# An adaLN attention and gated-mixer block on one core: projections stage with paired modulation sums, output projection with seven held tiles, mixing in the common ring

## The chip, the cores and the metric

The kernel runs on one core of one Trainium2 chip. The metric is the device time of one execution in microseconds (us); less is better. Three runs of the kernel before took 1479.3, 1481.84 and 1483.68 us, and their median, 1481.84 us, is the time that a change is held against.

## What is computed

The reference, cut to what matters (S = 2048 rows, D = 448 columns, 16 heads of 28, Fh = 896; all float32):

```python
mod = (silu(c) @ w_mod).reshape(1, 6, 1, D)          # sa, ca, ga, sb, cb, gb
h = layernorm(x) * (1 + ca) + sa
q, k, v = split_heads(h @ wqkv)
p = softmax(q @ k.T / sqrt(28))                      # per head, 2048 x 2048
x = x + ga * (merge_heads(p @ v) @ wo)
h = layernorm(x) * (1 + cb) + sb
z = gelu(h @ w_in)                                   # 2048 x 1792
z1, z2 = z[:, :Fh], layernorm(z[:, Fh:])
g = w_sp @ z2 + b_sp[:, None]                        # w_sp: 2048 x 2048
out = x + gb * ((z1 * g) @ w_out)
```

## The kernel before

The kernel is written with a manual schedule: on each engine the instructions run in the order in which the program issues them, and nothing reorders them. TensorE's operands are split into a high and a low part, so a float32 product is made of several single-pass matmuls. `weight_part` (L76) and `ln_transpose` (L96) make the parts: the high one by a cast on ScalarE or VectorE, the low one by a subtraction (`sub`, L69) on GpSimd or VectorE. A product over D = 448 takes the 11 steps of `STEPS` (L31): 9 of `STEPS_MAIN`, which need the columns 0 to 383, and 2 of `STEPS_Z`, which need the columns 384 to 447 (part c = 3).

Rows are handled in 16 tiles of 128, four to a group. The stages, in order:

1. **Projections** (L169 to L311). `x` is loaded group by group, `w_mod` in six column blocks (`load_mod`, L145), each turned into a sum over k on VectorE (`mod_acc`, L185) and into columns or a broadcast row by matmuls (`mod_col`, L193; `mod_bc`, L199). For each group, `ln_stats` and `ln_norm` (L206, L219) normalise on VectorE with the reciprocal root on GpSimd, `ln_transpose` transposes on TensorE, `v_tile` (L237) makes V, and `qk_unit` (L244) makes 128 rows of q or k for the group and stores their high and low parts in DRAM (`qk_scr`). Seven row blocks m of q and k times four groups make 28 such units; 8 of them (m = 0 and 3) run within the group loop.
2. **Start of attention.** When the group loop has ended, its memory is freed (`early.close()`), the tiles `kst` and `qst` for three heads are made, the rows of ones in `kst` are written by three DMAs (L330), and `load_head` (L334) reads the heads 0 and 1 from DRAM. 20 more `qk_unit`s follow. The first 4 have nothing between their matmuls; into the other 16, 80 score matmuls for the row maxima (`m_mm`, L343, each followed by a VectorE reduction of 512 columns, L351) are laid, 5 to a unit.
3. **Attention loop** over 256 steps u = (head, key tile): 4 score matmuls (`s_mm`, L374) with their exponentials on ScalarE, 4 `m_mm` for 20 steps later, and the products with V (`pv_mm`, L387). A softmax sum comes out as row 28 of each block of 32 rows. After each head `n_copy`, `n_sum`, `n_recip`, `n_bcast`, `n_mul` and `n_scatter` (L398 to L433) bring the sums through DRAM to a broadcast reciprocal, multiply, and put the head's rows into `OT`. For the last head this chain runs after the loop (`run_tail`).
4. **Output projection and second norm** (L555 to L670). The `STEPS_MAIN` of 12 tiles run first and are added to `x`, while the last head's chain runs; then `o_split` (L435) splits its rows and the `STEPS_Z` of these tiles follow in small batches, each with a second addition. Norms (`h2_stats`, `h2_norm`, L585, L595) and `h2_group` go in between; the last-written parts of each group's `ln_transpose` go to VectorE.
5. **First half of the gated layer**: 28 `z1_unit`s (L669), with the later groups' norms between them; then the **second half**, `z2_gemm` (L737) per tile.
6. **Mixing** (`mix_part`, L787): 1344 matmuls into seven accumulators, then `gate` (L807) and the output product `y_part` (L825).

PSUM has 8 banks. `ring` holds 7 of them, used in turn by all stages up to the mixing, and `ps_o` one. Before the mixing both are closed, and `ps_f` gives the eight banks fixed names (acc0 to acc6, y_ps).

SyncE issues nearly all DMAs, in program order; each issue also waits until the eighth DMA before it has landed.

Of the kernel before, what the change touches and what calls it, by code (L numbers as in the profile page):

```python
# [20 lines left out]
NG = 4  # L21
# [12 lines left out]
def tile_adaln_mha_gmlp(ctx, tc, x, wqkv, wo, w_in, w_spT, b_sp, w_out, cT, w_mod, out):  # L34
# [17 lines left out]
    dve.memset(ones, 1.0)  # L52
    mhalf = const.tile([128, 4], F32, name="mhalf")
# [42 lines left out]
    def ln_transpose(xns, full_pool, dsts, scol, bcol, engs, los=(pool,) * 4, mid=None):  # L96
# [9 lines left out]
        for c in (0, 2, 1, 3):  # L106
# [13 lines left out]
            if c < 3:  # L120
                sub(los[c], dsts[:, 3 + c, :], f, hi)
            else:
                sub(los[c], hi[64:128], f[64:128], hi[64:128])

# [14 lines left out]
    early = ExitStack()  # L139
    e1 = early.enter_context(tc.tile_pool(name="e1", bufs=2))  # L140

    wv = e1.tile([128, 8, D], F32R, name="wv", bufs=1)
    wms, xts, raws = {}, {}, {}

    def load_mod(i, nm, eng):  # L145
        wm = e1.tile([112, 4, D], F32, name="wm")
        eng.dma_start(wm, w_mod[:, i * D : (i + 1) * D].rearrange("(k p) d -> p k d", p=112))
        wms[nm] = wm

    def load_x(g, eng):  # L150
        xg = e1.tile([128, 4, D], F32, name="xg")
        for t0, t1 in ((0, 1), (1, 2), (2, 4)) if g == 0 else ((0, 4),):
            eng.dma_start(
                xg[:, t0:t1, :], x[g * 512 + t0 * 128 : g * 512 + t1 * 128].rearrange("(t p) d -> p t d", p=128)
            )
        for t in range(4):
            xts[4 * g + t] = xg[:, t, :]
# [13 lines left out]
    load_mod(1, "ca", sp)  # L171
    load_mod(0, "sa", sp)
    for i in range(4):
        load_w("v", i, sp)
# [10 lines left out]
    def mod_acc(nm):  # L185
        acc = e1.tile([112, D], F32, name="acc")
        wm = wms[nm]
        dve.tensor_scalar(out=acc, in0=wm[:, 0, :], scalar1=silu[:, 0:1], scalar2=None, op0=ALU.mult)
        for k in range(1, 4):
            dve.scalar_tensor_tensor(out=acc, in0=wm[:, k, :], scalar=silu[:, k : k + 1], in1=acc, op0=ALU.mult, op1=ALU.add)  # L190
        return acc

    def mod_col(nm, acc, plus1):  # L193
        pc = ps_o.tile([128, 512], F32, name="pc", tag="o")
        for c, r, e in ((0, 0, 128), (1, 0, 128), (2, 0, 128), (3, 0, 64), (3, 64, 128)):
            pe.matmul(pc[r:e, c : c + 1], acc[:, c * 128 : c * 128 + e - r], ones[:112, 0:1], start=True, stop=True)
        return lambda: dve.tensor_scalar(out=cols[nm], in0=pc[:, 0:4], scalar1=plus1, scalar2=None, op0=ALU.add)

    def mod_bc(nm, acc):  # L199
        pc = ps_o.tile([128, 512], F32, name="pc", tag="o")  # L200
        pe.matmul(pc[:, :D], ones[:112, :], acc, start=True, stop=True)
        dve.tensor_copy(bcs[nm], pc[:, :D])
# [34 lines left out]
    def v_tile(kt):  # L237
        g, t = divmod(kt, 4)
        pv = ring.tile([128, 512], F32, name="pv", tag="s")
        for j, (a, b) in enumerate(STEPS):  # L240
            pe.matmul(pv[:, :D], hT[g][:, a, t * 128 : (t + 1) * 128], wv[:, b, :], start=j == 0, stop=j == NST - 1)
        dve.tensor_copy(V[:, kt, :, 0:DH], pv[:, :D].rearrange("p (h d) -> p h d", d=DH))
# [16 lines left out]
    ln_stats(0)  # L259
    xns = ln_norm(0)  # L260
    acc_ca = mod_acc("ca")
    acc_sa = mod_acc("sa")
    for i in range(4):
        weight_part(wv, i, raws["v", i], act, pool, False)
    ad = (act, act, dve, dve)

    def mod_first():
        col_ca = mod_col("ca", acc_ca, 1.0)
        col_ca()
        mod_col("sa", acc_sa, 0.0)()  # L270

    ln_transpose(
        xns, e1, hT[0], cols["ca"], cols["sa"], ad, (pool, pool, dve, dve), mod_first,
# [4 lines left out]
    pool.memset(V[:, :, :, DH:32], 1.0)  # L278
    ln_stats(1)
    xns = ln_norm(1)  # L280
    for g in range(NG):
        if g + 2 < NG:
            load_x(g + 2, sp)
        if g == 0:
            load_mod(2, "ga", sp)
            load_mod(3, "sb", sp)
        v_tile(4 * g)
        v_tile(4 * g + 1)
        if g == 0:
            for i in range(4):  # L290
                weight_part(wqk, i, raws["qk", i], act, (dve, pool)[i % 2], False)
        if g + 1 < NG:
            ln_transpose(xns, e1, hT[g + 1], cols["ca"], cols["sa"], (act,) * 4)
        v_tile(4 * g + 2)
        if g == 3:
            mod_col("sb", acc_b, 0.0)()
            acc_b = mod_acc("gb")
        v_tile(4 * g + 3)
        if g == 3:
            mod_col("cb", acc_a, 1.0)()  # L300
        if g + 2 < NG:
            ln_stats(g + 2)
        for m in (0, 3):
            qk_unit(m, g)
        if g + 2 < NG:
            xns = ln_norm(g + 2)
        if g == 1:
            acc_a = mod_acc("ga")
            load_mod(4, "cb", sp)
            acc_b = mod_acc("sb")  # L310
            load_mod(5, "gb", sp)  # L311
        if g == 2:
            mod_bc("ga", acc_a)
            acc_a = mod_acc("cb")
        if g == 3:
            mod_bc("gb", acc_b)
    early.close()


    stk = att.enter_context(tc.tile_pool(name="stk", bufs=1))  # L320
    ppool = att.enter_context(tc.tile_pool(name="ppool", bufs=6))
    kst = [stk.tile([128, S], F32R, name=f"kst{i}") for i in range(3)]
    qst = [stk.tile([128, S], F32R, name=f"qst{i}") for i in range(3)]
    npool = att.enter_context(tc.tile_pool(name="npool", bufs=2))
# [3 lines left out]

    for i in range(3):
        sp.dma_start(  # L330
# [578 lines left out]
```

## Time and profile before

| | us |
|---|---|
| median of three runs | 1481.84 (1479.3 to 1483.68) |
| the profiled execution | 1484.28 |
| its span, from the first to the last instruction | 1482.5 |
| TensorE matmul busy in it | 1444.3 |
| VectorE, ScalarE, GpSimd busy | 891.8, 723.7, 294.2 |
| mean granted TensorE clock | 0.994 of full |

The page of the profile gives the busy time of each engine (PE is TensorE's matmuls, PEld its weight loads, DVE VectorE, ACT ScalarE, POOL GpSimd, SP SyncE, SPq its DMA issues), then 40 equal slices of the span. Other views group instructions by line, list who waited for whom, give the busy time in chosen stretches, or list instructions in order of time: start, duration, engine, line, operation, count, and in brackets the idle time before it and what ended it. Busy matmuls are modelled to the end of their pipeline, so that neighbours overlap; the distance between starts is the real pace.

### The profile page before, as it was taken

What the parts mean: (1) busy time and instruction counts of PE and PEld (TensorE: products, weight loads), DVE (VectorE), ACT (ScalarE), POOL (GpSimd) and SP (SyncE); (2) the same over time, 40 slices, a digit from 0 to 9 for tenths busy, and PEclk for the clock granted to TensorE, in tenths of its full rate; (3) what the DMA queues carried; (4) which work ended last, traced back from release to release, by engine and by line L of the source; (5) the groups of instructions that cost most, each with busy time, mean ns of one, the idle gap of its engine ahead of it and who ended that gap; (6) DMA issues with size and microseconds to landing.
All of it is one profiled execution on the core that took longest, in us unless ns stands there. A gap on an engine that the chain in (4) does not pass through costs nothing. (4 is left out here: it accounts for less than half of the span.)

```text
span 1482.5 us, 19584 instructions
## 1 busy us (share of the span) xinstructions
PE 1444.3 (97%) x7284; PEld 1014.8 (68%) x7284; DVE 891.8 (60%) x1469; ACT 723.7 (49%) x1374; POOL 294.2 (20%) x282
## 2 busy tenths in 40 slices
PE   4998999999999999999999999999999999999999
PEld 3886755555555555555555547778988888888887
DVE  6726888888888888888888821752541411413114
ACT  3522467677677676776776784343432210211111
POOL 4723300000002011101000021540763300302002
PEclk8999999999999999999999999999999999999999
DMA  9336402210122112221022004632003322323223
GB/s 233 107 108 203 151 17 52 52 41 25 40 52 52 39 35 57 52 48 43 16 51 52 12 20 122 206 111 100 8 21 102 114 75 68 106 62 101 84 68 106
DMA packets 58790, 111.57 MB, mean 75 GB/s; under 512 B 12006, under 2 KB 27462, under 8 KB 56006
## 3 DMA queue, kind: packets, MB, share of 16 engines
q1 hardware_dynamic: 58534, 109.40, 25.9%
q8 instruction: 57, 0.93, 0.3%
q0 software_dynamic: 160, 0.92, 0.2%
q14 instruction: 39, 0.32, 0.1%
HBM read 76.15 MB, written 29.49 MB: 71 GB/s over the span
## 5 line engine op out<-in xcount | busy, mean ns | idle before, releaser
L351 DVE TENSOR_REDUCE pm<-mt 128x1 f32<-128x512 f32 x1024 | 628.1, 682 | 131.0 <-PE mt L346 129.8
L381 ACT ACTIVATE P<-st_ps 128x512 f32<-128x512 f32 x1024 | 514.2, 620 | 153.7 <-PE st_ps L377 153.3
L377 PE MATMUL st_ps<-qst,kst 86*128 86x512 f32 x1024 | 409.8, 411 | 0.0
L346 PE MATMUL mt<-kst,qst 84*128 84x512 f32 x1024 | 400.7, 397 | 5.2 <-DMA qst<-qk_scr 3.2
L377 PEld LDWEIGHTS st_ps<-qst,kst 86*128 86x128 f32 x1024 | 192.8, 189 | 145.1 <-issue 80.5
L392 PE MATMUL o_ps<-P,V 128*32 128x512 f32 x2048 | 247.5, 598 | 0.0
L346 PEld LDWEIGHTS mt<-kst,qst 84*128 84x128 f32 x1024 | 194.6, 190 | 45.0 <-DVE pm L351 4.5
L70 DVE TENSOR_TENSOR wsp_l<-raw_sp,wsp_h 128x512 fp32r<-128x512 f32 x64 | 48.7, 763 | 193.0 <-ACT wsp_h L727 193.0
L727 ACT ACTIVATE wsp_h<-raw_sp 128x512 fp32r<-128x512 f32 x64 | 40.4, 631 | 248.6 <-DMA raw_sp<-in_w_spT_dram 170.9
L392 PEld LDWEIGHTS o_ps<-P,V 128*32 128x32 f32 x2048 | 54.1, 109 | 123.1 <-issue 116.2
L70 POOL TENSOR_TENSOR heapD<-u,heapD 128x512 fp32r<-128x512 f32 x27 | 44.6, 1685 | 261.2 <-ACT heapD L811 261.2
L418 POOL TENSOR_TENSOR osb<-osb,rb 128x512 f32<-128x512 f32 x16 | 20.4, 1277 | 366.3 <-DMA rb<-r_scr 220.7
L792 PE MATMUL acc<-wsp_h,heapD 128*128 128x512 f32 x224 | 89.2, 398 | 2.9 <-ACT zg L747 1.6
L794 PE MATMUL acc<-wsp_h,heapD 128*128 128x512 f32 x224 | 88.5, 395 | 0.0
L793 PE MATMUL acc<-wsp_l,heapD 128*128 128x512 f32 x224 | 88.3, 394 | 0.0
L249 PE MATMUL pq<-heapD 128*128 128x512 f32 x308 | 79.8, 398 | 0.0
L249 PEld LDWEIGHTS pq<-heapD 128*128 128x128 f32 x308 | 58.6, 191 | 13.6 <-issue 0.4
L70 POOL TENSOR_TENSOR nl<-nf,nh 16x128 fp32r<-16x128 f32 x16 | 7.2, 451 | 272.8 <-issue 180.6
L672 PE MATMUL z_ps<-heapB,heapA 128*128 128x512 f32 x231 | 54.5, 396 | 0.0
L744 PE MATMUL z_ps<-heapD,heapB 128*128 128x448 f32 x264 | 53.0, 363 | 0.0
L837 DVE TENSOR_TENSOR x2t<-x2t,y_ps 128x448 f32<-128x448 f32 x12 | 7.5, 621 | 75.7 <-PE y_ps L834 75.7
L744 PEld LDWEIGHTS z_ps<-heapD,heapB 128*128 128x128 f32 x264 | 49.6, 188 | 3.3
(156 smaller groups left out, 1629.0 us busy)
## 6 DMA issues: line engine op xcount, KB each, us to landing
raw_sp<-in_w_spT_dram SPq DMA_DIRECT2D x64, 256.0 KB
kst<-qk_scr SPq DMA_DIRECT2D x48, 224.0 KB
qst<-qk_scr SPq DMA_DIRECT2D x48, 224.0 KB
qk_scr<-qh SPq DMA_DIRECT2D x28, 256.0 KB
qk_scr<-ql SPq DMA_DIRECT2D x28, 256.0 KB
z_scr<-z1t SPq DMA_DIRECT2D x28, 256.0 KB
z<-z_scr SPq DMA_DIRECT2D x28, 256.0 KB
wm<-in_w_mod_dram SPq DMA_DIRECT2D x6, 784.0 KB
```

What stands on the lines that cost most here:

```text
L70: eng.tensor_tensor(out=dst, in0=a, in1=hi.bitcast(F32), op=ALU.subtract)
L249: pe.matmul(pq, wqk[:, b, m * 128 : (m + 1) * 128], hT[g][:, a, :], start=j == 0, stop=j == NST - 1)
L346: pe.matmul(mt, qst[h % 3][0:84, t * 128 : (t + 1) * 128], kst[h % 3][0:84, kb * 512 : (kb + 1) * 512], start=True, stop=True)
L351: dve.tensor_reduce(out=pms[h][:, t, kb : kb + 1], in_=mt, axis=AX.X, op=ALU.max)
L377: pe.matmul(st, kst[h % 3][0:86, kt * 128 : (kt + 1) * 128], qst[h % 3][0:86, qb * 512 : (qb + 1) * 512], start=True, stop=True)
L381: act.activation(p, st, AF.Exp, scale=SCALE)
L392: pe.matmul(otile[h][32 * qb : 32 * qb + 32, :], V[:, kt, h, :], ptiles.pop((u, qb)), start=kt == 0, stop=kt == NT - 1)
L672: pe.matmul(ps_t, w1[:, b, f * 128 : (f + 1) * 128], h2T[g][:, a, :], start=j == 0, stop=j == NST - 1)
L744: pe.matmul(ps_t[:, :D], h2T[g][:, a, tt * 128 : (tt + 1) * 128], w2[:, b, hf * D : (hf + 1) * D], start=j == 0, stop=j == NST - 1)
L792: pe.matmul(acc[f], z2[st][:, 0, fs], hi, start=st == 0, stop=False)
L793: pe.matmul(acc[f], z2[st][:, 0, fs], lo, start=False, stop=False)
L794: pe.matmul(acc[f], z2[st][:, 1, fs], hi, start=False, stop=st == NT - 1)
```

## The change

It edits five places.

- **Inputs.** `x` and `w_mod` are laid out on the host so that a partition's part of a load is contiguous: up to 7168 bytes for a group of `x` (before: four pieces of 1792), 3584 bytes for one k of a pair of `w_mod` blocks.
- **Projections.** The six modulation blocks become three pairs of 112x2x448 tiles, summed by 12 VectorE instructions of 896 columns in place of 24 of 448. `mod_col` and `mod_bc` use `ring` banks. Matmuls that compute nothing needed (`pe_fill`: 4, then 10) stand around the first `mod_col`. Weight parts 1 and 3 of `wv` are made between the parts of the first `ln_transpose`. In group 0, tiles 0 and 1 alternate their matmuls, and tile 2 comes ahead of the next group's transposes. `ln_stats` and `ln_norm` of group g+2 move ahead of the last V tiles of group g.
- **Start of attention.** In group 3 the memory is freed first, ones are written by GpSimd memsets, the first 1536 columns of head 0 are loaded ahead of the group's two `qk_unit`s and the rest behind them; its four V tiles follow. All 20 later `qk_unit`s carry 4 score matmuls each, those that need only the first 1536 columns first.
- **Output projection.** One matmul with a selection matrix `spread` broadcasts the last head's sums to the rows that need them; VectorE takes the reciprocal of 128x512 and multiplies; the chain through DRAM is gone, and the 8 scatter DMAs are issued by SyncE and ScalarE, 4 each. Seven tiles run `STEPS_MAIN` and keep their banks until the `STEPS_Z` follow; the other nine run all 11 steps at once, and each is added once. The norms and groups stand in a new order, the second norm's parts are all made on ScalarE and GpSimd, and its 64 repeated columns come from VectorE instead of GpSimd copies. The four `w_in` blocks are loaded together at the stage's start. `z1` results go through four buffers in place of two.
- **Mixing.** `ring` and `ps_o` stay open; accumulators are `ring` tiles, and one more block of `w_sp` is loaded ahead.

The diff, cut to its core:

```diff
+    dve.tensor_copy(spread..., ident...[:, :, 28:29].broadcast_to([128, 4, 32]))
...
+    def load_mod(pair, eng):
+        for k in range(4):
+            wms[pair, k] = e1.tile([112, 2, D], F32, name="wm", bufs=4)
+            eng.dma_start(wms[pair, k], w_mod[:, pair, k])
...
+    wu = ring.tile([128, 512], F32, name="wu", tag="s")
+    def pe_fill(n):
+        for _ in range(n):
+            pe.matmul(wu[:, 0:128], ones, ones, start=True, stop=True)
...
     ln_stats(0)
+    mod_acc(0, 0)
+    mod_acc(0, 1)
     xns = ln_norm(0)
-    acc_ca = mod_acc("ca")
-    acc_sa = mod_acc("sa")
+    mod_acc(0, 2)
+    mod_acc(0, 3)
...
     def mod_first():
-        col_ca = mod_col("ca", acc_ca, 1.0)
-        col_ca()
-        mod_col("sa", acc_sa, 0.0)()
+        pe_fill(4)
+        mod_col(("ca", accs[0][:, 1, :], 1.0), ("sa", accs[0][:, 0, :], 0.0))
+        pe_fill(10)
...
+        if g == 3:
+            early.close()
+            ...
+            load_head(0, 0, 1536)
+            for m in (0, 3):
+                qk_unit(m, g)
+            load_head(0, 1536, S)
         if g == 0:
+            v_tiles(0, 1)
+            v_tiles(2)
...
         if g + 1 < NG:
             ln_transpose(xns, e1, hT[g + 1], cols["ca"], cols["sa"], (act,) * 4)
-        v_tile(4 * g + 2)
...
         if g + 2 < NG:
             ln_stats(g + 2)
+            xns = ln_norm(g + 2)
+        if g > 0:
+            v_tiles(4 * g + 2)
+        v_tiles(4 * g + 3)
...
+        if g in (1, 2):
+            for k in range(4):
+                mod_acc(g, k)
...
+    first = sorted(((t, kb) for t in range(NT) for kb in range(4)), key=lambda a: (max(a[0] // 4, a[1]) // 3, a))
...
     for i, (m, g) in enumerate((m, g) for m in (4, 1, 5, 2, 6) for g in range(NG)):
-        if i < NQ:
-            qk_unit(m, g)
-        else:
-            n = 2 * LEAD * (i + 1 - NQ) // (20 - NQ) - mh[0]
-            qk_unit(m, g, {j: m_half for j in ((4, 9) if n == 2 else (1, 5, 9))})
+        qk_unit(m, g, {j: m_first for j in (1, 4, 7, 10)})
...
+    HELD = 7
     x_load(0)
+    for i in range(4):
+        win_load(0, i)
+    wo_mm(0, STEPS_MAIN)
+    sums = ps_o.tile([128, 512], F32, name="sums", tag="o")
+    pe.matmul(sums, spread, osb[h], start=True, stop=True)
+    rb = stage.tile([128, 512], F32, name="rb", tag="qh")
+    dve.reciprocal(rb, sums)
+    dve.tensor_tensor(out=osb[h], in0=osb[h], in1=rb, op=ALU.mult)
+    n_scatter(h)
+    for g in range(1, 4):
+        x_load(g)
+    for i in range(2):
+        win_prep(0, i, pool)
+    for t in range(1, HELD):
+        wo_mm(t, STEPS_MAIN)
+    for qb in range(4):
+        o_split(3, qb, dve if qb % 2 == 0 else pool)
+    ...
+    for t in range(HELD):
+        wo_mm(t, STEPS_Z)
+        wo_add(t)
+    h2_stats(0)
+    wo_tile(7)
+    h2_stats(1)
+    h2_norm(0)
...
+    for t in (8, 9, 10):
+        wo_tile(t)
+    h2_norm(1)
+    wo_tile(11)
+    h2_group(0)
+    h2_stats(2)
+    wo_tile(12)
+    wo_tile(13)
+    h2_norm(2)
+    h2_group(1)
+    wo_tile(14)
+    wo_tile(15)
+    h2_stats(3)
...
-    ps.close()
...
-            acc[f] = ps_f.tile([128, 512], F32, name=f"acc{f}")
+            acc[f] = ring.tile([128, 512], F32, name="acc", tag="s")
```

## The prediction

> **What bounds the kernel now.** I read the page's busy times and slices first, then the stages one by one, then what TensorE waited for. From the page:
>
> ```profile
> PE 1444.3 (97%) x7284; PEld 1014.8 (68%) x7284; DVE 891.8 (60%) x1469; ACT 723.7 (49%) x1374; POOL 294.2 (20%) x282
> ...
> PE   4998999999999999999999999999999999999999
> ```
>
> TensorE is the bound in every slice but the first three or four. So a change that leaves its matmuls as they are can win only where it idles or runs at a lower clock. The stages, from the view of busy times in stretches (length, then busy time and count of PE, PEld, DVE, ACT, POOL, then the granted clock, DMA share, GB/s):
>
> ```profile
> 0.00:42.10 42.10, 21.96 (x96) 18.15 (x97) 30.27 (x50) 13.84 (x20) 23.20 (x31) 0.88 0.82 208
> 42.10:111.40 69.30, 66.99 (x325) 57.39 (x324) 34.14 (x58) 25.78 (x40) 33.34 (x33) 0.98 0.38 114
> 111.40:177.10 65.70, 60.76 (x254) 47.13 (x254) 50.52 (x80) 20.66 (x35) 22.25 (x18) 1.00 0.53 175
> 177.10:905.10 728.00, 727.74 (x4033) 412.45 (x4031) 581.16 (x976) 529.90 (x1071) 61.09 (x68) 1.00 0.17 41
> 905.10:1025.40 120.30, 116.24 (x549) 98.75 (x549) 59.32 (x106) 40.76 (x61) 40.54 (x44) 0.99 0.47 157
> ...
> 1097.60:1482.50 384.90, 379.92 (x1680) 315.04 (x1680) 99.21 (x139) 62.09 (x99) 68.39 (x46) 1.00 0.28 87
> ```
>
> They are: projections up to the first q/k unit, the rest of the group loop, the units with score matmuls, attention, output projection with z1, and, behind the second half of the gated layer, mixing. Attention (728 of 1482.5 us) has no idle time and the change leaves its order alone. What can move lies at its two ends. TensorE's waits:
>
> ```profile
> PE tp L103 <- DVE xn L224: 14.2, 2, 12.6
> PE mt L346 <- DMA qst<-qk_scr: 3.2, 1, 3.2
> ...
> PE acc L792 <- ACT zg L747: 1.6, 1, 1.6
> PE mt L346 <- DVE pm L351: 1.6, 2, 0.8
> ```
>
> Columns: who waited for whom, us in total, times, longest.
>
> **1. The start, up to the first q/k unit.** Rows in order of time:
>
> ```profile
> 9.02 1.15 DVE L211 BATCH_NORM_STATS2 st<-xg 128x6 f32<-128x448 f32 x2 [3.94 <-DMA xg<-in_x_dram]
> ...
> 12.03 1.78 DVE L224 TENSOR_SCALAR xn<-xg,mv,rs 128x448 f32<-128x448 f32 x4 [1.57 <-POOL rs L94]
> ...
> 12.60 4.30 PE L103 MATMUL tp<-ident,xn 128*128 128x128 f32 x16 [12.60 <-DVE xn L224]
> ...
> 14.21 2.12 DVE L190 SCALAR_TENSOR_TENSOR acc<-wm,silu,acc 112x448 f32<-112x448 f32 x3
> ...
> 16.69 1.28 PE L196 MATMUL pc<-ones,acc 112*128 112x1 f32 x10
> ...
> 20.83 0.16 DVE L197 TENSOR_SCALAR col_sa<-pc 128x4 f32<-128x4 f32 x1 [1.14 <-PE pc L196]
> ...
> 37.80 4.25 DVE L70 TENSOR_TENSOR heapD<-raw,heapD 128x896 fp32r<-128x896 f32 x1
> ...
> 42.14 5.15 PE L249 MATMUL pq<-heapD 128*128 128x512 f32 x22
> ```
>
> The chain is: x lands (9.0), statistics, norm (12.0 to 13.8), modulation sums on VectorE, col_sa (21.0), group 0's parts, group 1's norm, the q/k weights' low parts on VectorE (to 42.05), first unit (42.14). How fast do loads get with longer contiguous rows?
>
> ```profile
> 8.00:12.00 4.00, 0.00 (x0) 0.00 (x0) 1.43 (x6) 0.00 (x0) 1.28 (x2) 1.00 1.06 230
> 24.00:26.00 2.00, 1.66 (x5) 1.51 (x6) 1.90 (x4) 1.94 (x3) 0.45 (x1) 0.50 1.04 348
> ```
>
> In the first stretch all rows in flight are of 1792 bytes (448 floats), in the second most are of 3584 (the 896-column weights). If that is the cause, the last piece of x lands about 2 us earlier. VectorE then has the statistics done near 8.2, takes two paired sums of at most 1.4 us (2.12 / 3 x 2; the first, without an addend, is shorter), the norm until 12.5 and two more sums until 15.3, against 19.6 now. TensorE still does 16 transposes, which end 4.3 us after their start near 11, 4 fill and 20 small column matmuls (about 0.8 and 2.5); so col_sa comes near 18.5, 2.5 earlier. Everything behind it is the same chain on the same engines: VectorE's c = 2 and 3, norm 1, V copies, then the two low parts, which are slow beside GpSimd (4.25 us above) where the same form takes 1.09 later:
>
> ```profile
> L70 DVE TENSOR_TENSOR heapD<-raw_in,heapD 128x896 fp32r<-128x896 f32 x3 | 3.3, 1092 | 3.0 <-ACT heapD L81 3.0
> ```
>
> So the first unit moves by as much as col_sa. Ends: -5 (all loads at 348 GB/s, and VectorE undisturbed) and +1 (loads unchanged; the two sums ahead of the norm cost up to 2.8 and cover the 1.57 of waiting for the root). I take **-2.5**. The ten other fill matmuls run while ScalarE makes the first part, and tile 2 ahead of the transposes fills a wait for norm 1; if that cover is gone, they cost their own 1 to 2 us.
>
> On the loads the Trainium skill's "DMA: Bandwidth & Descriptors" (Specifications) speaks against me: it puts the least transfer for line rate at 512 bytes, so that 1792 is as good as 3584. By it this term would be about -1 (only the sums' new place is left) and the whole 1.5 us less; the two stretches above, 230 and 348 GB/s, speak for the other reading, though they differ in more than row length. It is rival R1.
>
> **2. From the first unit to attention, 42.1 to 177.1 (135.0 us).** What would this work take without gaps? Starts of the TensorE rows:
>
> ```profile
> 47.13 4.68 PE L241 MATMUL pv<-wv,heapD 128*128 128x448 f32 x22
> 51.65 1.91 PE L103 MATMUL tp<-ident,xn 128*128 128x128 f32 x16
> 53.31 4.76 PE L241 MATMUL pv<-wv,heapD 128*128 128x448 f32 x22
> ...
> 73.91 3.27 PE L241 MATMUL pv<-wv,heapD 128*128 128x448 f32 x11 [2.31 <-DVE V L242]
> 76.97 6.09 PE L249 MATMUL pq<-heapD 128*128 128x512 f32 x22
> ...
> 75.00:79.00 4.00, 4.00 (x14) 3.35 (x13) 0.62 (x1) 0.00 (x0) 0.81 (x1) 0.57 0.61 185
> ```
>
> From starts, 22 V matmuls take 4.52 us (0.205 each), 16 transposes 1.66, 22 q/k matmuls 4.99 (42.14 to 47.13; 0.227). In 42.1 to 111.4 lie 136 q/k (30.9), 132 V (27.1), 32 transposes (3.3) and 2.5 of small ones: 63.9 against 69.3. The 5.4 us are the 2.3 for V's copy (mod_acc held VectorE), the half-clock stretch at 75 to 79 behind it (about 1.7), and slower pitches. In 111.4 to 177.1 stand 172 q/k and 80 score matmuls; at the even pitch late in the stretch, 0.233, they take 58.8 against 65.7: 3.2 for head 0's load, 1.6 for reductions, 2 of half-filled ring. Together 12.3 us are idle or slow.
>
> What takes these away?
>
> ```profile
> L351 DVE TENSOR_REDUCE pm<-mt 128x1 f32<-128x512 f32 x1024 | 628.1, 682 | 131.0 <-PE mt L346 129.8
> ```
>
> Head 0's load was late by 3.2 us behind four units (44 x 0.227 = 10.0 us), so it took 13.2 from the group loop's end. Now it starts at the beginning of group 3, needs no store of that group for its first 1536 columns, and has two units and four V tiles in front of its first reader (5.0 + 9.0 us). Four score matmuls per unit mean 4 x 0.682 = 2.7 us of reductions beside 15 x 0.233 = 3.5 of TensorE, so the 1.6 goes. V copies no longer queue behind sums: the four paired ones (up to 4 x 1.4, perhaps twice that beside GpSimd) fall under the group's two units (5.0) and the next V tile. What is late next: norm g+2 stands ahead of V copies and waits for GpSimd's root, which waits behind four subtractions; the ring's seven banks cover that, and without them TensorE would wait as at 73.9, 2 us a group. The three memsets of ones fall on GpSimd, which is busy 22 of 66 us there. I recover 8.5 of 12.3: **-8.5** (bounds -12, and -4 if only the two waits of 3.2 and 2.3 go and a new one of 1.5 comes).
>
> **3. Output projection and z1, 905.1 to 1025.4.** Rows:
>
> ```profile
> 905.10 30.46 PE L561 MATMUL wo_ps<-heapD 128*128 128x448 f32 x149
> 935.39 2.92 PE L103 MATMUL tp<-ident,x 128*128 128x128 f32 x16
> ...
> 1008.00 17.62 PE L672 MATMUL z_ps<-heapC,heapA 128*128 128x512 f32 x77
> 1025.45 4.79 PE L744 MATMUL z_ps<-heapD,heapB 128*128 128x448 f32 x23
> ```
>
> Without gaps: 176 x 0.203 = 35.8, four sets of transposes 6.6, 308 x 0.228 = 70.2; 112.6 against 120.35, so 7.7 to gain. The risk is the wait of the held tiles for the last head's rows. What bears on it, three rows in order of time and four of groups:
>
> ```profile
> 82.90 0.92 PE L201 MATMUL pc<-acc,ones 112*128 112x448 f32 x2
> ...
> 920.39 6.99 SPq L429 DMA_DIRECT2D heapD<-osb  x8
> ...
> 925.07 0.63 ACT L444 ACTIVATE zt<-heapD 128x512 fp32r<-128x512 f32 x1 [14.29 <-DMA heapD<-osb]
> ```
>
> ```profile
> L408 DVE RECIPROCAL rt<-rt 128x16 f32<-128x16 f32 x16 | 3.9, 244 | 45.3 <-DMA rt<-osb 45.3
> ...
> L182 DVE RECIPROCAL ec<-ec 112x4 f32<-112x4 f32 x1 | 0.2, 178 | 0.0
> ```
>
> ```profile
> L110 ACT ACTIVATE hfull<-tp,col_sb,col_cb 128x512 f32<-128x512 f32 x8 | 6.2, 776 | 9.2 <-DMA z_scr<-z1t 5.1 <-POOL heapB L70 4.0
> ```
>
> The sums' matmul is new, 0.92 / 448 x 512 = 1.05 us. The held tiles' 63 matmuls and it end at 905.1 + 12.8 + 1.05 = 918.9. The sums are there at 908.0 (behind tile 0's nine). A reciprocal of 512 columns is in no row: 12 more columns cost 66 ns, 5.5 a column, so 3.0 us; floor 0.7 (the 512-column reduction), ceiling 7.8 (244 / 16 a column). I take 3.0, the slope between its own two rows. Product 0.7 to 1.1: 912. The first split came 4.7 us after the scatter's first issue, so 916.7; but 2.7 MB of x and w_in go ahead of the scatter, 8 us at 348 GB/s from 906.5. With ScalarE's two weight casts, its four issues and a split of 0.63 + 0.63 ahead of the first Z matmul: 918 to 921. So a wait of about 1 us, bounds 0 and 8. SyncE's x loads 1 to 3 stand behind the scatter and are first needed by tile 4's addition, near 921. ScalarE alone makes the second norm's parts, four of 0.776 + 0.63 a group, 5.6, while two to four projection tiles of 2.2 run. Sum: -7.7 + 1.05 + 1 + 1.65 for what the new order of norms may leave: **-4** (bounds -6.5 and +2).
>
> **4. Mixing.** The 1.6 us wait for the old banks goes, since ring banks come free one by one: **-1.6** (bounds 0 and -2.9).
>
> Sum: -2.5 - 8.5 - 4 - 1.6 = -16.6. From the profiled execution's 1484.28 that is 1467.7; from the median of the runs, 2.4 lower, 1465.2. I give **1466**.
>
> **Rivals.** R1, loads gain nothing from row length: 1466 + 1.5 = 1467.5; against it the 348 GB/s.
>
> R2, waits change places: VectorE beside GpSimd still sets the q/k weights, group 3 waits for its freed memory, the held tiles wait 3 to 4 us and the clock halves for a while, as at 75 us. Half of terms 1 to 3 is left: 1482 - 7.5 - 1.6 = 1473. For it: the 4.25 us row; against it: TensorE had no such wait wherever ring banks were free.
>
> R3, gaps were slack: attention's own pace, VectorE's 581 us of 728 with reductions of 0.68, gives the start's gain back. Then 3 and 4 alone stay, about 1476. Against it: TensorE is busy 727.74 of 728.0.
>
> R4, slower: head 0's load becomes the wait. It cannot start until the last modulation sum and the last transposes leave the freed memory, and SyncE holds all later stores behind it, so q/k buffers fill. Each us beyond the 14 that cover it costs one, and a stretch at half clock as at 75 us adds 1.7. From about 14 us late on (1481.8 - 1466 - 1.7) it eats the whole gain; at 20 late it gives 1466 + 20 + 1.7 = 1488. For it: the load was late before; against it: it took 13.2 then, and the sums take under 11 us.
>
> **How the numbers follow.** Forecast 0.47 (its own range 1460 to 1470), R1 0.15, R2 0.22, R3 0.08, R4 0.08. The sum of the good ends is -26 (1456), of the bad ones +1 - 4 + 2 = -1 (1481). I leave R4 and the last us of either end out: 1457 to 1477. About 0.3% (4.4 us) is what a measurement of this kernel can tell from no change; all but R4 and the worst of R2 and R3 lie beyond it: faster 0.87, same 0.05, slower 0.08.
>
> **What would show it.** Right: the first q/k unit near 39.5; no PE wait over 1 us until attention, which starts near 166 and lasts 728; z1 ends 114 to 117 us after attention; no wait at the first accumulator. Wrong: a wait of score matmuls for kst or qst, PE idle near 919 for over 4 us, attention longer than 732, or a reciprocal far from 3.0 us.

## The result, and the profile after

The changed kernel takes **1469.1 us** (median of 4 runs, 1467.87 to 1470.85); its ratio to the kernel before is **0.9916, 95% interval 0.99 to 0.9931**. The forecast was 1466, in a range of 1457 to 1477. (One run of the kernel before, disturbed, is not in the ratio.) The profiled execution took 1468.3 us against 1484.28, 16.0 less; the medians differ by 12.7, because the profiled execution of before was 2.4 above its median and that of the changed kernel 0.8 below.

The profile's page of the changed kernel: TensorE has 3.4 us less of busy time with 30 more matmuls, and no slice behind the first with a tenth to spare.

```profile
PE 1440.9 (98%) x7314; PEld 1016.6 (69%) x7314; DVE 882.5 (60%) x1440; ACT 733.0 (50%) x1390; POOL 301.3 (21%) x273
...
PE   6999999999999999999999999999999999999999
```

The same stages as before, in the view of busy times in stretches (columns as in the prediction): until group 0's two q/k units are through, until attention, attention, output projection with z1, mixing.

```profile
0.00:45.40 45.40, 28.76 (x146) 24.21 (x147) 29.36 (x57) 16.62 (x24) 29.64 (x34) 0.96 0.67 194
45.40:165.30 119.90, 119.57 (x556) 100.05 (x555) 79.10 (x121) 43.31 (x70) 57.20 (x50) 1.00 0.50 160
165.30:893.10 727.80, 727.78 (x4033) 413.10 (x4031) 581.04 (x975) 529.85 (x1071) 61.08 (x68) 1.00 0.17 41
893.10:1012.30 119.20, 114.95 (x551) 97.99 (x551) 53.03 (x88) 50.79 (x77) 39.16 (x32) 1.00 0.46 157
...
1082.80:1466.50 383.70, 379.37 (x1681) 315.12 (x1679) 102.14 (x141) 63.12 (x100) 71.31 (x49) 1.00 0.28 87
```

Against before: 47.1 became 45.4, 130.0 became 119.9, attention kept its 728, 120.35 became 119.3, and the last stretch lost 1.1 (384.84 to 383.7); z2, between the last two lines, went from 72.2 to 70.4. So the gain lies in the second line, and output projection, where 4 were expected, gave 1. What TensorE still waits for:

```profile
PE tp L109 <- DVE xn L243: 13.0, 1, 13.0
PE pq L270 <- DVE heapD L76: 2.9, 1, 2.9
PE wo_ps L600 <- POOL heapD L76: 1.8, 1, 1.8
PE tp L109 <- DVE x L639: 1.5, 1, 1.5
PE wo_ps L600 <- ACT zt L487: 1.0, 1, 1.0
```

The waits for head 0's load (3.2), for V's copy (2.3) and for the old banks (1.6) are gone. So is the longest wait of the output projection before, for an addition, which the prediction did not list:

```profile
PE wo_ps L561 <- DVE xl L581: 2.6, 1, 2.6
```

New in the changed kernel are the second line (the first q/k unit waits for its weights' low parts) and lines 3 to 5 (output projection). The rows behind them are a selection in order of time, first from the start, then from the output projection:

```profile
8.32 1.15 DVE L230 BATCH_NORM_STATS2 st<-xg 128x6 f32<-128x448 f32 x2 [3.02 <-DMA xg<-in_x_dram]
...
13.02 4.31 PE L109 MATMUL tp<-ident,xn 128*128 128x128 f32 x16 [13.02 <-DVE xn L243]
17.12 1.92 PE L195 MATMUL wu<-ones 128*128 128x128 f32 x8
18.82 1.96 PE L212 MATMUL pc<-ones,acc 112*128 112x1 f32 x20
20.91 0.15 DVE L216 TENSOR_SCALAR col_sa<-pc 128x4 f32<-128x4 f32 x1
...
33.39 6.00 DVE L76 TENSOR_TENSOR heapD<-raw,heapD 128x896 fp32r<-128x896 f32 x2
39.44 6.15 PE L270 MATMUL pq<-heapD 128*128 128x512 f32 x19 [2.93 <-DVE heapD L76]
...
895.01 1.02 PE L673 MATMUL sums<-osb,spread 128*128 128x512 f32 x2
...
905.44 4.66 POOL L76 TENSOR_TENSOR heapA<-wraw,heapA 128x896 fp32r<-128x896 f32 x2 [32.81 <-ACT heapA L87]
908.22 1.86 PE L600 MATMUL wo_ps<-heapD 128*128 128x448 f32 x8 [1.04 <-ACT zt L487]
910.18 1.60 POOL L76 TENSOR_TENSOR heapD<-heapD,zt 64x512 fp32r<-64x512 f32 x1
911.83 12.62 PE L600 MATMUL wo_ps<-heapD 128*128 128x448 f32 x61 [1.76 <-POOL heapD L76]
...
920.67 3.19 DVE L639 TENSOR_SCALAR x<-x,mv,rs 128x64 f32<-128x64 f32 x8 [0.88 <-POOL rs L100]
...
925.36 7.33 DVE L639 TENSOR_SCALAR x<-x,mv,rs 128x64 f32<-128x64 f32 x8
...
926.51 2.70 POOL L76 TENSOR_TENSOR heapB<-hfull,heapB 128x512 fp32r<-128x512 f32 x2 [4.54 <-ACT heapB L123]
...
932.75 1.42 PE L109 MATMUL tp<-ident,x 128*128 128x128 f32 x11 [1.45 <-DVE x L639]
```

Each wait shows its queue. GpSimd makes two low parts of w_in (905.44, 4.66 us) and so begins the second split only at 910.18; the Z matmuls of the tiles behind it start at 911.83. Norm 1 takes VectorE 7.33 us, while GpSimd subtracts beside it from 926.51 on, where norm 0's same eight instructions (920.67) took 3.19.

### The profile page after: what moved, and what is told of

Same layout as the page of the kernel before. It is cut to its first block, busy times and chain, and to the rows that moved or that the text cites. A ratio compares the mean times of both kernels' runs of the same rounds, so it can differ in the third digit from the quotient of the medians.

```text
span 1466.5 us, 19636 instructions
## 1 busy us (share of the span) xinstructions
PE 1440.9 (98%) x7314; PEld 1016.6 (69%) x7314; DVE 882.5 (60%) x1440; ACT 733.0 (50%) x1390; POOL 301.3 (21%) x273
## 4 chain that ended last, share of the span: by engine, by line
PE 94%; DVE 2%; DMA 2%; issue 1%; POOL 1%; SPq 0%; ACT 0%; DVEq 0%; POOLq 0%; ACTq 0%
PE st_ps L420 18%; PE mt L389 16%; PE o_ps L435 16%; PE acc L820 7%; PE acc L822 7%; PE acc L821 7%; PE pq L270 5%; PE z_ps L774 5%; PE z_ps L712 5%; PE pv L261 2%; PE y_ps L861 2%; PE y_ps L862 2%; PE y_ps L860 2%; PE tp L109 1%; DMA wm<-in_w_mod_dram 1%
## 5 line engine op out<-in xcount | busy, mean ns | idle before, releaser
L389 PE MATMUL mt<-kst,qst 84*128 84x512 f32 x1024 | 405.8, 396 | 0.3 <-DVE pm L394 0.3
L76 DVE TENSOR_TENSOR wsp_l<-raw_sp,wsp_h 128x512 fp32r<-128x512 f32 x64 | 52.2, 818 | 188.7 <-ACT wsp_h L757 188.7
L270 PE MATMUL pq<-heapD 128*128 128x512 f32 x308 | 87.4, 402 | 2.9 <-DVE heapD L76 2.9
L270 PEld LDWEIGHTS pq<-heapD 128*128 128x128 f32 x308 | 59.2, 193 | 17.1 <-DVE heapD L76 3.4
L272 ACT ACTIVATE qf<-pq 128x512 f32<-128x512 f32 x28 | 16.7, 597 | 66.9 <-PE pq L270 66.9
L820 PEld LDWEIGHTS acc<-wsp_h,heapD 128*128 128x128 f32 x224 | 42.1, 188 | 10.9 <-DVE u L837 1.8
L822 PEld LDWEIGHTS acc<-wsp_h,heapD 128*128 128x128 f32 x224 | 42.1, 188 | 10.4
```

Of the source, the lines that this page charges most:

```text
L76: eng.tensor_tensor(out=dst, in0=a, in1=hi.bitcast(F32), op=ALU.subtract)
L270: pe.matmul(pq, wqk[:, b, m * 128 : (m + 1) * 128], hT[g][:, a, :], start=j == 0, stop=j == NST - 1)
L389: pe.matmul(mt, qst[h % 3][0:84, t * 128 : (t + 1) * 128], kst[h % 3][0:84, kb * 512 : (kb + 1) * 512], start=True, stop=True)
L820: pe.matmul(acc[f], z2[st][:, 0, fs], hi, start=st == 0, stop=False)
L822: pe.matmul(acc[f], z2[st][:, 1, fs], hi, start=False, stop=st == NT - 1)
```

## The experiments

All are measured against the kernel before on the same chip. "Attention" is the start of the first score matmul of its loop, "projection" the output projection with z1, both from the profiled execution (before 177.1 and 120.35, changed 165.3 and 119.28).

| kernel | median us | ratio, 95% | attention | projection |
|---|---|---|---|---|
| x in rows of 1792 bytes | 1470.85 | 0.9938 [0.9923, 0.9953] | 166.3 | 119.3 |
| no fill matmuls | 1466.74 | 0.9903 [0.989, 0.9916] | 164.6 | 117.7 |
| before + ring in mixing | 1480.34 | 0.9999 [0.999, 1.0008] | 174.9 | 118.9 |
| old spacing | 1472.68 | 0.9945 [0.9933, 0.9957] | 167.7 | 119.2 |
| old spacing, late load | 1475.77 | 0.9969 [0.9959, 0.998] | 173.0 | 119.1 |
| w_in prepared first | 1468.45 | 0.9921 [0.9907, 0.9936] | 166.7 | 117.2 |
| norm 1 earlier | 1467.42 | 0.9914 [0.9898, 0.993] | 166.5 | 117.4 |
| low parts on VectorE | 1472.0 | 0.9947 [0.9934, 0.996] | 169.1 | 118.6 |
| the same, x(3) earlier | 1465.29 | 0.989 [0.9875, 0.9905] | 162.9 | 119.0 |
| x(3) earlier alone | 1468.56 | 0.9912 [0.9895, 0.9928] | 165.6 | 119.9 |
| all that helped | **1461.28** | **0.9867 [0.985, 0.9884]** | 161.9 | 115.8 |
| before + paired start | 1479.76 | 0.9998 [0.9986, 1.0011] | 175.1 | 119.8 |

The third line shows how far parts that are not touched vary: its start and its projection are those of before, and it has 174.9 against 177.1 and 118.9 against 120.35.

**Row length.** x is laid out as the kernel before had it, and `x_load` reads it in the same way:

```
-            eng.dma_start(xg[:, t0:t1, :], x[g, :, t0:t1])
+            eng.dma_start(
+                xg[:, t0:t1, :], x[g * 512 + t0 * 128 : g * 512 + t1 * 128].rearrange("(t p) d -> p t d", p=128)
+            )
```

> The changed kernel with x in its natural layout (every row of a load 1792 bytes again, in the first loads and in the output projection); the order of instructions stays. Theory (row length set the load): the last piece of x lands at 9.0 to 10.3 us instead of 8.3, and the first V tile and attention begin 0.7 to 2 us later; 1470 to 1471. Rival (row length is worth nothing, x came earlier because less was queued beside it): x lands at 8.3, attention begins at 165.3 as in the changed kernel, 1469.

x's last piece came at 8.22 instead of 8.32, and nothing in the output projection moved. The rival holds for x: row length is not what brings it. In the profiled execution attention begins 1.0 later because 19 matmuls run at a lower clock (7.3 us instead of 6.0; granted clock 0.50 instead of 0.65 from 40 to 44 us). The intervals of the two ratios overlap.

**Fills.** Both calls of `pe_fill` are taken out.

> The changed kernel without the 14 fill matmuls. Theory (the four in front of the column sums are on the path): the column matmuls start at 17.1 instead of 18.8, the modulation columns are there near 19.0, and everything behind is up to 1.9 us earlier; 1467.3. Rival (the fills hold the clock): the granted clock halves somewhere between 20 and 38 us, as in the kernel before, and the first q/k unit is no earlier or 1 to 2 us later; 1469 to 1471.

Rows in order of time, the column matmuls and the first V tile:

```profile
16.86 3.26 PE L206 MATMUL pc<-ones,acc 112*128 112x1 f32 x20
...
21.99 1.49 PE L255 MATMUL pv<-wv,heapD 128*128 128x448 f32 x3 [1.87 <-ACT heapD L123]
```

The column matmuls start 2 us earlier, as the theory said, but take 3.26 us instead of 1.96. Why is not shown: in the last experiment, which has no fills either, the same 20 take 1.91. From the last statistics to the first V tile stay 14.03 us against 14.65: 0.6 gained, not 1.9. The rival's drop of the clock did not come: it is 1.00 in every stretch from 12 to 36 us without a fill, so nothing here shows that the fills hold it. The ratio's interval overlaps that of the changed kernel.

**Mixing alone**, in the kernel before:

```
-    ps.close()
-    ps_f = ctx.enter_context(tc.tile_pool(name="ps_f", bufs=1, space=PSUM))
-            acc[f] = ps_f.tile([128, 512], F32, name=f"acc{f}")
+            acc[f] = ring.tile([128, 512], F32, name="acc", tag="s")
...
```

> The kernel before with one part of the change alone: accumulators and y of the mixing in the ring and the single bank, no pools closed and opened ahead of it. Theory (the price was the wait for the old banks): the wait of the first accumulator for the last gelu (1.6) goes and nothing else moves; the profiled stretch from the first z2 to the end is 1.6 shorter than 457.1, and the median 1481. Rival (the whole 2.9 that this end of the kernel gained comes from the ring, for example because y no longer shares its bank): 454.2 for that stretch, median 1480. Rival (worth nothing): 457.1, 1482.8.

From the first z2 to the first accumulator it takes 70.43 us (1022.05 to 1092.48) instead of 72.21: the wait of 1.6 is gone, and every profiled kernel with the ring has that 70.43. Mixing itself took 385.3, no less than before; in the others it is 383.2 to 385.1 without any edit to it. So 1.8 of the profile's 2.9 is this part, the rest the spread of mixing. The median does not show the 1.8; the interval's lower end is 0.999. Why it does not stays open.

**Spacing, and head 0's load.** The score matmuls are spaced as before:

```
-        qk_unit(m, g, {j: m_first for j in (1, 4, 7, 10)})
+        qk_unit(m, g, {j: m_first for j in ((), (1, 3, 5, 7, 9))[i >= 4]})
```

> The changed kernel with the score matmuls of the first head spaced as before: the first four of the last 20 q/k units have none, the others five. Theory (even spacing was worth about half of the 3.6 us of reductions and half-filled ring): 16 units with 5 x 0.68 = 3.4 us of reductions beside 3.6 of TensorE, so waits for the reductions come back; attention begins 1.5 to 3 us later, 1470.6 to 1472. Rival (the early load did it all): attention begins at 165.3 and the time is 1469.

For the late load, besides that, `load_head(0)` stands behind the group loop and group 3's units m = 0 and 3 behind its V tiles again.

> The changed kernel with the old spacing of the score matmuls and head 0 loaded behind the group loop, as in the kernel before; group 3's two q/k units stand behind its V tiles again, so the stores that the load waits for come last. Theory (the load needs about 13 us from the loop's end and four empty units cover 10): a wait of 3 us for the loaded rows at the first score matmul, on top of what the old spacing costs; 1473 to 1475. Rival (the load is hidden anyway): no such wait, same time as with the old spacing alone.

The waits of both, the old spacing first, then with the late load:

```profile
PE mt L389 <- DVE pm L394: 1.3, 4, 0.3
```

```profile
PE pv L261 <- DVE V L263: 3.1, 1, 3.1
...
PE mt L384 <- issue: 2.5, 1, 2.5
PE mt L384 <- DVE pm L389: 1.2, 4, 0.3
```

Old spacing brings 1.3 us of waits for reductions back and starts attention 2.4 later; the late load brings a wait of 2.5 at the first score matmul, near the 3 expected, and the time between the two ratios is 0.24%, 3.6 us. (The profile names no releaser for this wait, `issue`; it stands where the kernel before waits for the load.) Both theories hold in the profile, and both times lie 0.7 to 0.8 above their ranges. Not all of the 3.6 is the load: of the 5.3 us by which its attention begins later, 2.8 are there at 76 us already, behind the wait of 3.1 for V's copy, which has another cause, next but one.

**w_in first, norm 1 earlier.** The two changes of order in the output projection:

```
+    for i in range(2):
+        win_prep(0, i, pool)
     wo_mm(0, STEPS_MAIN)
...
-    for i in range(2):
-        win_prep(0, i, pool)
```

(with the four `win_load` ahead of `x_load(0)`), and

```
-    for t in (8, 9, 10):
-        wo_tile(t)
-    h2_norm(1)
+    wo_tile(8)
+    h2_norm(1)
+    for t in (9, 10):
+        wo_tile(t)
```

> The changed kernel with the four loads of w_in ahead of that of x, and the first two preparations of w_in (ScalarE casts, GpSimd low parts) ahead of the last head's product and scatter. Theory (the held tiles' two waits, 1.0 and 1.8 us, come from ScalarE's and GpSimd's work on w_in standing between the scatter and the splits): both waits go, the first split comes 1.8 earlier, output projection and z1 take 117 instead of 119.3; 1466.5. Rival (the scatter's DMAs set it, or the second norm does): the wait turns up under another name, 119.3, 1469. Third way: w_in lands after 900.3, the casts hold ScalarE's four scatter issues back, and the waits grow; 1471.

> The changed kernel with the second norm of group 1 ahead of the additions of projection tiles 9 and 10 on VectorE. Theory (the 1.45 us wait of the transposes is VectorE's queue): norm 1 starts 1.0 us earlier, the wait falls to 0.5, 1468. Rival (banks held by tiles 9 to 11 take its place): TensorE waits for a bank by as much or more; 1469 to 1471.

The held tiles with w_in first, and the transposes of norm 1 in the kernel without fills, where neither edit was made:

```profile
908.20 14.48 PE L600 MATMUL wo_ps<-heapD 128*128 128x448 f32 x69 [0.56 <-ACT heapD L489]
```

```profile
929.68 2.23 PE L109 MATMUL tp<-ident,x 128*128 128x128 f32 x16
```

w_in first leaves 0.6 of the held tiles' 2.8 us of waiting and takes 117.2. GpSimd begins the second split 2.2 us earlier in the stage (14.9 instead of 17.1 us after its start), as the theory has it. The first split does not come earlier (13.0 in both): it now waits for the scatter's DMAs, as the rival has it. Norm 1 earlier starts that norm 1.0 us earlier in the stage, takes 4.04 us for it instead of 7.33, and leaves no wait of the transposes; the stage takes 117.4. That wait, however, is absent without the edit too, in the kernels without fills, with old spacing, with low parts on VectorE and with x(3) earlier alone, so this run does not show that the edit removed it. Nor is either told from the changed kernel in the time: in the kernels that leave the stage as it is, it takes 117.7 to 119.9.

**Low parts of the q/k weights.** VectorE makes all four:

```
-weight_part(wqk, i, raws.pop(("qk", i)), act, (dve, pool)[i % 2], False)
+weight_part(wqk, i, raws.pop(("qk", i)), act, dve, False)
```

> The changed kernel with the low parts of all four q/k weights on VectorE instead of two on GpSimd. Theory (the two engines hold each other up: 3.0 us each for two at a time, where VectorE alone takes 1.09): with GpSimd's parts gone VectorE is through its four in 4.4 to 7 us, from 33.4 to 38 to 40, and the 2.9 us wait of the first q/k unit falls to 0 to 1.5; 1467 to 1468. Rival (GpSimd then makes the other group's low parts at the same time, so VectorE is as slow as before, 3 us each): 12 us, the first unit waits until 45 instead of 39.4; 1474.

Neither answer: the weights came sooner than hoped, and the kernel got slower. Its rows, and the clock behind the new wait:

```profile
33.32 4.08 DVE L76 TENSOR_TENSOR heapD<-raw,heapD 128x896 fp32r<-128x896 f32 x4
...
50.22 0.40 SPq L162 DMA_DIRECT2D xg<-in_x_dram  x1
...
56.66 2.21 DVE L230 BATCH_NORM_STATS2 st<-xg 128x6 f32<-128x448 f32 x4 [8.99 <-DMA xg<-in_x_dram]
...
64.53 6.21 DVE L206 SCALAR_TENSOR_TENSOR acc<-wm,silu,acc 112x896 f32<-112x896 f32 x3
65.61 7.62 POOL L76 TENSOR_TENSOR heapD<-hfull,heapD 128x512 fp32r<-128x512 f32 x4
...
71.33 4.47 PE L261 MATMUL pv<-wv,heapD 128*128 128x448 f32 x11 [4.78 <-DVE V L263]
```

```profile
72.00:76.00 4.00, 4.00 (x12) 3.49 (x11) 0.49 (x2) 0.00 (x0) 1.23 (x1) 0.52 0.49 133
```

Four low parts take 4.08 us where two took 6.00, and group 0's units end at 40.9 instead of 45.4. But SyncE issues group 3's load of x at 50.2, as in the changed kernel (50.8), because it stands behind the stores of q/k low parts, which GpSimd is late with. Its statistics wait 8.99 us for it, norm and sums follow, and V's copies at 70.7. TensorE, now 4.5 us ahead, stands 4.78 at V and then runs 4 us at a clock of 0.52. The three sums also take longer than in the changed kernel:

```profile
64.32 4.44 DVE L206 SCALAR_TENSOR_TENSOR acc<-wm,silu,acc 112x896 f32<-112x896 f32 x3
```

There GpSimd's subtractions for the next group begin at 67.89, behind the sums; here TensorE's earlier transposes bring them to 65.61, beside the sums, and V's copies come 2.0 us later than in the changed kernel (70.66 against 68.68). So a faster start is given back here, and more than that. The new theory is that the load of x for group 3, not the start, sets the group loop's pace.

```
-        if g + 2 < NG:
-            load_x(g + 2, sp)
+        if g == 0:
+            load_x(2, sp)
...
+        if g == 0:
+            load_x(3, sp)
         if g < 3:
             for m in (0, 3):
```

> The changed kernel with all four low parts of the q/k weights on VectorE (which by itself brought the end of group 0's units from 45.4 to 40.9 and gave it all back in a wait of 4.8 for V's copies at 71) and group 3's load of x issued ahead of group 0's q/k stores on SyncE instead of behind them. Theory (SyncE holds that load until the stores of the low parts, 50.2 whatever the start does, and so VectorE's norm 3, modulation sums and V copies come at a fixed time): the load lands before 47, the sums start near 59.5 instead of 63.5, the wait for V falls from 4.8 to under 1, attention begins at 160 to 162 instead of 169.1, time 1464 to 1465. Rival (the sums are slow beside GpSimd, 7 us wherever they stand, and hold V's copies in any case): a wait of 3 us or more stays and attention begins at 165 or later, 1468 or more.

> The changed kernel with the earlier load of x for group 3 alone, the low parts of the q/k weights shared as in the change. Theory (in the changed kernel TensorE reaches V's copies just after VectorE, with no wait, so the load has no one to help): attention begins at 165.3 plus or minus the spread of the start (0.7), 1468 to 1469. Rival (the group loop runs in step with that load): attention 2 us or more earlier.

Rows of the first of the two in order of time, and its wait for V:

```profile
33.49 0.44 SPq L162 DMA_DIRECT2D xg<-in_x_dram  x1
...
61.16 5.45 DVE L206 SCALAR_TENSOR_TENSOR acc<-wm,silu,acc 112x896 f32<-112x896 f32 x3
```

```profile
PE pv L261 <- DVE V L263: 0.9, 1, 0.9
```

The load goes out at 33.5, the sums start at 60.1, the wait is 0.9, and attention begins 6.2 earlier than with the low parts alone, at 162.9, which is 0.9 later than the theory's 160 to 162; with the low parts shared, the same edit moves attention by 0.3. Both are as the theories have it in kind: two bounds stood at one place, and only moving both pays. The sums still take 5.45, with GpSimd subtracting beside their last part (from 64.36), and V's copies stand behind them.

**All that helped.** The fills are out, the low parts on VectorE, x(3) early, w_in first, and norm 1 earlier.

> The changed kernel with what the single experiments point to: no fill matmuls, all low parts of the q/k weights on VectorE, group 3's x ahead of the q/k stores, the first two preparations of w_in ahead of the last head's scatter, norm 1 of the second half two tiles earlier. If the gains add up: 0.8 from the fills and 4.5 from the weights (attention begins at 160), 2 from w_in's preparations and 0.5 to 1 from the norm (output projection and z1 116 to 117): 1461 to 1462. Rival (each only moves the next wait): one of the two ends stays where it was, 1464 to 1467.

Stretches of the best kernel as above, up to the end of z1, and its held tiles:

```profile
0.00:40.40 40.40, 25.57 (x119) 22.08 (x120) 27.01 (x57) 14.82 (x22) 23.27 (x29) 1.00 0.79 222
40.40:161.90 121.50, 120.28 (x557) 99.80 (x556) 80.05 (x122) 44.87 (x73) 60.03 (x54) 1.00 0.49 157
...
889.70:1005.40 115.70, 115.05 (x551) 97.92 (x551) 50.42 (x88) 50.97 (x77) 39.07 (x32) 1.00 0.47 161
```

```profile
892.08 26.16 PE L594 MATMUL wo_ps<-heapD 128*128 128x448 f32 x123
```

The gains add up in the time: 1461.28, below both kernels and inside the 1461 to 1462 expected, though attention begins at 161.9, not at 160. All 123 matmuls of held and first whole tiles run in one piece where the changed kernel has three, and output projection with z1 takes 115.8, inside the 114 to 117 of the prediction and below the 117.7 to 119.9 of the kernels that leave it as it is.

**The start alone**, in the kernel before: paired sums, two ahead of the norm, both columns in one bank; `w_mod`'s first two blocks come in four loads instead of two.

```
+    pair_acc(0)
+    pair_acc(1)
     xns = ln_norm(0)
-    acc_ca = mod_acc("ca")
-    acc_sa = mod_acc("sa")
+    pair_acc(2)
+    pair_acc(3)
```

> The kernel before with one part of the change alone: the first two modulation sums paired (896 columns at once), two of the four ahead of the first norm, both columns in one bank; x's layout, weights and everything behind stay, no fill matmuls. Theory as the traces so far have it (the columns come at 20.2 in the changed kernel without fills, at 20.8 and 22.2 in two executions of this start as it was): col_sa at 20 to 20.5, first V tile near 22, the end of group 0's units within the spread of the two executions, 44.8 to 47.1; 1480 to 1482. Rival (the start's part is worth its 2.5 us as the prediction had it): col_sa at 18.5, first q/k unit's pair through at 43 or earlier, and 2.5 us of the total, ratio 0.998 or less.

Rows in order of time, the wait for head 0's load, and V's wait in the other execution of the old start (the kernel with the ring in mixing):

```profile
7.12 1.15 DVE L232 BATCH_NORM_STATS2 st<-xg 128x6 f32<-128x448 f32 x2 [1.24 <-DMA xg<-in_x_dram]
...
18.05 0.15 DVE L223 TENSOR_SCALAR col_sa<-pc 128x4 f32<-128x4 f32 x1
...
69.56 3.66 PE L262 MATMUL pv<-wv,heapD 128*128 128x448 f32 x11 [2.29 <-DVE V L263]
```

```profile
PE mt L367 <- issue: 4.0, 1, 4.0
```

```profile
71.62 2.52 PE L241 MATMUL pv<-wv,heapD 128*128 128x448 f32 x11 [2.31 <-DVE V L242]
```

The columns came at 18.05, as the rival (the prediction's own number, 18.5) had it. But of the 2.8 us gained on the profiled execution of before, 1.9 are x, whose last piece came at 7.12 instead of 9.02 in the same rows; from there to col_sa it took 10.9 us, and 11.8 and 13.5 in the two executions of the old start. (SyncE issues the fourth piece of `wv` only when x has landed, at 7.11, where the kernel before issued it at 5.79. That fewer loads beside it brought x earlier is not shown.) Group 0's units were through at 42.7, against 47.1 and 44.8.

The time did not move. Against the execution with 44.8 the lead of 2.1 is still there when V's wait ends (69.56 against 71.62), so this wait, 2.3 in both, does not absorb it. The 11 matmuls behind it take 1.1 longer, at a clock of 0.57 (70 to 74 us) instead of 1.00, and the wait at the first score matmul is 4.0 instead of 3.3; attention begins at 175.1, against 174.9. Both readings fail in part: the start did get faster, and what stood behind it took the gain back.

## Why the prediction was right, step by step

**What bounds the kernel** was right: the gains came from TensorE's idle and slow time at the two ends of attention, and attention kept its 728 us (R3 is out).

**Term 1 (-2.5; measured -1.7 between the two profiled executions)** came near by luck. The old start had group 0's units through at 47.1 in one execution and at 44.8 in the other, and the changed kernel's 45.4 lies between. The step "if that is the cause", row length, failed: x came at 8.2 with either layout, and at 7.1 with the old one in the last experiment. By the Trainium skill's "DMA: Bandwidth & Descriptors" (Specifications), cited in the prediction as rival R1, 1792 bytes are as good as 3584; the trace agrees, 8.22 us against 8.32, and R1's reading of the loads held. So x's last piece came 0.7 earlier, not 2, VectorE waited 0.9 us between the first two sums for `w_mod`, and the transposes began at 13.0, not "near 11". As the fills and column matmuls ("about 0.8 and 2.5") took 1.7 and 1.9 from start to start, col_sa stayed at 20.9. The first unit's wait of 2.93 for the weights, which R2 named ("VectorE beside GpSimd still sets the q/k weights"), is the new bound.

**Term 2 (-8.5; measured -10.1)** was right in kind and a little small; the other execution of the old kernel has the same 130 us there. Of its parts, spacing is worth 2.4 at attention's start; moving the load back brings a wait of 2.5, and its share of the 3.6 in the time is not told apart. R4 did not happen: no wait for the load of head 0 is left.

**Term 3 (-4; measured -1.1)** is the step that failed. It did not fail for the reasons given as uncertain: the reciprocal took 3.36 us (3.0 forecast), the sums' matmul 0.46 from start to start (1.05). "A wait of about 1 us" for the held tiles was 2.8 in two pieces, and of the "1.65 for what the new order of norms may leave" 1.45 appeared as a wait. The prediction priced ScalarE's casts ahead of the splits, and the first piece, 1.04, is of that size; it priced neither GpSimd's two low parts ahead of the second split (4.66 us) nor VectorE's norm beside GpSimd (7.33 instead of 3.19). With both queues moved, among other edits, the stage takes 115.8, 4.6 less than before, so the 4 could be had; 3.1 of the 7.7 are left. Since the stage varies by up to 2.2 between kernels that leave it as it is, -1.1 itself is known no better than that.

**Term 4 (-1.6; measured -2.9)**: the wait is worth 1.8 in the profile, and the rest is spread. In the time, this part alone shows nothing (0.9999).

**The sum** of -16.6 stands against -16.0 between the two profiled executions, but -12.7 between the medians, so it came out in part by luck. The choice of the profiled executions flatters the terms: against the other execution of the old start and projection, terms 1 and 3 are +0.6 and +0.4 instead of -1.7 and -1.1, which is of the size of the 3.3 between -16.0 and -12.7 and of the 3 by which 1469.1 exceeds 1466. And what term 4 has beyond the wait, 1.1, belongs to no edit.

Of the marks given, attention near 166 (165.3) and no wait at the first accumulator held; the first unit near 39.5 held for most of it (3 matmuls at 35.65, 19 from 39.44); no PE wait over 1 us until attention, and z1's end after 114 to 117, did not. R2's time, 1473, was too slow by 4, but two of the waits that it names (q/k weights, held tiles) are in the profile.

## What to carry to other kernels

A stage's end is set by a chain and by fixed times beside it: before a start is made faster, ask which DMA issue or which engine's queue arrives at the same place at a time that does not move with it. Where a wait is predicted from one engine, go through every queue that feeds the waiting instruction and count what stands ahead of it there, the halves made by a slower engine too. Ask also whether an earlier start moves one engine's work beside another's that it slows down. An edit that gains nothing alone can pay once the second bound beside it is moved, so try the two together.

## What the runs showed of the hardware

- **The price of the same gap differs from execution to execution.** Behind the same wait of 2.9 us, the same 19 matmuls took 4.44 us (old spacing with late load), 5.8 to 6.1 (five kernels) or 7.3 (two). The clock (sixth value, granted share) in the changed kernel and in the one with the late load:

```profile
40.00:44.00 4.00, 4.00 (x13) 3.18 (x12) 1.78 (x7) 2.25 (x4) 3.46 (x5) 0.65 0.01 4
```

```profile
40.00:44.00 4.00, 4.00 (x20) 3.38 (x19) 1.09 (x6) 3.00 (x5) 3.47 (x4) 1.00 0.20 71
```

  So a gap of 2.9 us cost 0, 1.5 or 3 us more behind it. The Trainium skill's "TensorE: Matmul & The Clock Gate" (Part 1) has the clock fall after an idle window of about 3.4 us whose phase is free; a spread of the price fits a free phase, but here gaps of 2.3 (0.57 behind V's wait in the last experiment, 1.00 behind the same wait in the kernel with the ring in mixing) and 2.9 us were enough.
- **VectorE beside GpSimd.** An 896-column subtraction took VectorE 3.00 us with GpSimd subtracting weights beside it (6.00 / 2) and 1.02 where VectorE made all four parts (4.08 / 4). GpSimd began its next subtraction at 35.65, beside the third of these four; there it was GpSimd's that took longer, 2.91 us instead of 1.29. The Trainium skill's "GPSIMD Engine Reference" (Specifications) says that the two engines contend when a VectorE instruction has two inputs in SBUF; the trace agrees, 3.00 us against 1.02. Two of the four parts beside GpSimd's weights took VectorE longer, by 1.9 us, than all four did without them.
- **A reciprocal** of 128 x 512 from PSUM took 3358 ns, 6.6 ns a column, against 695 ns for the product behind it.
